# V of block 2 from raw rows, blocks 2 and 3 transposed by DMA from ScalarE's queue, block 3 loaded earlier

## The chip, the core and the metric

The kernel runs on one core of one Trainium2 chip. The metric is the device time of one execution in microseconds. An engine here is one of the core's: TensorE (PE, with its weight loads shown apart as PEld), VectorE (DVE), ScalarE (ACT), GpSimd (POOL) and SyncE (SP, which only issues transfers). All five run their own instruction lists in order and wait for one another by semaphores.

## What is computed

x has 2048 rows of 512 values. Two branches read the layer-normalised rows and are added to x.

```
xn = layernorm(x)
A:  q, k, v = xn @ wqkv           # 32 heads of 16
    for every row s and head: 8 logits, with rows s, s-2, ... s-14; softmax; weighted sum of v
    A = o @ wo
B:  z  = gelu(xn @ w_in)          # 1792 columns
    z1 = z[:, :896];  z2 = layernorm(z[:, 896:])
    g  = w_sp @ z2 + b_sp         # over the rows
    B = (z1 * g) @ w_out
out = x + A + B
```

## The kernel before

The rows are cut into 16 blocks of 128 (b = 0 to 15). For each block VectorE takes mean and variance (`bnst`, `bnag`, `vpe`: lines 599, 601, 609), GpSimd the reciprocal root (`rstd`, line 611), VectorE the normalised rows (`norm`, line 623). TensorE needs the normalised rows transposed (`xnT`). For blocks 0 to 3 (`NXT = 4`) TensorE transposes them itself by four small matmuls with an identity (`xTr`, line 579) and ScalarE copies the result out of PSUM (`xTe`, line 587). Blocks 4 to 15 are transposed by a DMA that SP issues (`xTd`, line 617).

From `xnT` come V (two pairs of matmuls a block, `V2_0` and `V2_1` for block 2, line 654), z2 (eight matmuls of 448 columns a block, `z2_2_0`, `z2_2_1`, line 766, followed by ScalarE's gelu `z2g`, line 774, which empties their two PSUM banks), and for groups j of four blocks Q and K (line 677), z1 (line 812). So Q and K of j = 0 need blocks 0 to 3 transposed.

Blocks 0 and 1 have a way round the wait for the norm: their V is computed from the raw rows. TensorE transposes the raw rows (`xTx`, also line 579), ScalarE copies them (`xTc`, line 606), and V of the raw rows is mended afterwards with the column sums of the weights (`cs`, line 638, copied by `cse`, line 642): VectorE adds mean times minus the column sum into the PSUM bank (`fix`, line 660), and ScalarE's `Ve` (line 663) scales by rstd, reorders into the head order and empties the bank. GpSimd's queue writes V to DRAM (`Vw`, line 668), from where it is read much later in shifted copies.

The order is made in two steps. Every operation is a task with an estimated cost and a priority; `schedule` runs a list scheduler on those estimates and on the landing times given for the first loads (`land`), and so fixes each engine's instruction list and the PSUM banks. There are eight banks, and `place` gives a task that needs two of them an even pair (0,1), (2,3), (4,5) or (6,7), once all users of the banks' last contents have been scheduled; a matmul group then waits for those users. Hand-written chains (lines 1003 to 1012) force parts of the order at the start: on TensorE, VectorE and ScalarE. A task that only issues a DMA is counted with 0.48 us on its engine (`issue`, line 128).

SP loads at the start, in its order: wv in two halves, x2, the two halves of w_in's second part (`ldwin2a`, `ldwin2b`, lines 524 and 530), x3 to x7, wq, wk, x8 to x15. ScalarE's queue loads x0 and x1.

## Time and profile before

| | |
|---|---|
| time, median of 3 runs | 237.26 us (237.21 to 237.38) |
| profiled execution, first to last instruction | 236.1 us |
| the rest of the time around the span (difference of the two) | 1.2 us |
| PE busy | 231.7 us (98%) |
| DVE busy | 207.4 us (88%) |
| ACT busy | 96.5 us (41%) |
| granted TensorE clock | 1.000 |

Times inside the span count from its first instruction. The busy time of TensorE is the sum of its matmuls, in which the end of each is modelled; where matmuls follow each other without a break, the start of the next is the better mark. In a list of instructions in order of time, the columns are start, duration (both in us), engine, line, operation, output and input, shape, how many instructions were merged, and in brackets the idle time before and what ended it.

### The profile page before, as it was taken

What the parts mean: (1) busy time and instruction counts of PE and PEld (TensorE: products, weight loads), DVE (VectorE), ACT (ScalarE), POOL (GpSimd) and SP (SyncE); (2) the same over time, 40 slices, a digit from 0 to 9 for tenths busy, and PEclk for the clock granted to TensorE, in tenths of its full rate; (3) what the DMA queues carried; (4) which work ended last, traced back from release to release, by engine and by line L of the source; (5) the groups of instructions that cost most, each with busy time, mean ns of one, the idle gap of its engine ahead of it and who ended that gap; (6) DMA issues with size and microseconds to landing.
All of it is one profiled execution on the core that took longest, in us unless ns stands there. A gap on an engine that the chain in (4) does not pass through costs nothing.

```text
span 236.1 us, 2974 instructions
## 1 busy us (share of the span) xinstructions
PE 231.7 (98%) x1114; PEld 109.1 (46%) x1135; DVE 207.4 (88%) x269; ACT 96.5 (41%) x145; POOL 32.7 (14%) x56
## 2 busy tenths in 40 slices
PE   8999999999999999999999999999999999999996
PEld 3455555555444444444444444444444444444443
DVE  3799899999998899999699998986989997999432
ACT  3598889888967895510120531111111111000000
POOL 2259650311733100000000000000000000000000
PEclk9999999999999999999999999999999999999999
DMA  7998969991048325430999999998995959936432
GB/s 211 352 283 163 243 146 217 195 202 44 22 165 260 92 85 69 104 118 0 226 347 252 225 266 180 200 304 187 346 258 175 261 161 303 193 95 181 135 96 69
DMA packets 82013, 43.86 MB, mean 186 GB/s; under 512 B 54336, under 2 KB 81360, under 8 KB 82000
## 3 DMA queue, kind: packets, MB, share of 16 engines
q1 hardware_dynamic: 80768, 41.27, 71.5%
q0 software_dynamic: 800, 2.11, 2.8%
q10 hardware_dynamic: 432, 0.30, 0.6%
q8 instruction: 9, 0.15, 0.3%
q14 instruction: 4, 0.03, 0.1%
HBM read 26.35 MB, written 4.21 MB: 129 GB/s over the span
## 4 chain that ended last, share of the span: by engine, by line
PE 94%; DMA 3%; SPq 1%; ACT 1%; issue 1%; DVE 0%
PE ps L907 41%; PE ps L677 12%; PE ps L972 10%; PE ps L812 10%; PE ps L766 9%; PE ps L963 6%; PE ps L654 5%; DMA arena<-in_B_w_in_dram 3%; PE ps L713 1%; ACT arena L774 0%; SPq L518 0%; ACT arena L587 0%; PE ps L579 0%; SPq L514 0%; SPq L524 0%
## 5 line engine op out<-in xcount | busy, mean ns | idle before, releaser
L907 PE MATMUL ps<-arena 128*128 128x512 bf16 x439 | 96.6, 379 | 0.5
L907 PEld LDWEIGHTS ps<-arena 128*128 128x128 bf16 x448 | 43.7, 98 | 53.1 <-issue 0.4
L915 ACT ACTIVATE arena<-ps 128x1024 bf16<-128x1024 f32 (+1 forms) x16 | 14.7, 917 | 78.0 <-PE ps L907 78.0
L698 DVE TENSOR_TENSOR arena<-arena 128x4096 bf16<-128x4096 bf16 x16 | 36.5, 2282 | 0.1
L935 DVE TENSOR_TENSOR arena<-arena 128x4096 bf16<-128x4096 bf16 x16 | 36.4, 2283 | 0.0
L938 DVE TENSOR_TENSOR arena<-arena 128x2048 bf16<-128x2048 bf16 (+1 forms) x32 | 29.9, 948 | 0.0
L677 PE MATMUL ps<-arena 128*128 128x512 bf16 x126 | 28.7, 379 | 0.1
L703 DVE TENSOR_TENSOR arena<-arena 128x4096 bf16<-128x4096 bf16 x12 | 27.4, 2287 | 0.1
L972 PE MATMUL ps<-arena 128*128 128x512 bf16 (+2 forms) x117 | 26.9, 366 | 0.1
L766 PE MATMUL ps<-arena 128*128 128x448 bf16 x128 | 26.0, 352 | 0.5 <-DMA arena<-in_B_w_in_dram 0.5
L812 PE MATMUL ps<-arena 128*128 128x512 bf16 x110 | 24.4, 379 | 0.1
L978 DVE TENSOR_TENSOR arena<-ps,arena 128x512 bf16<-128x512 f32 (+2 forms) x17 | 11.2, 658 | 11.7 <-PE ps L972 11.7
L677 PEld LDWEIGHTS ps<-arena 128*128 128x128 bf16 x128 | 14.5, 113 | 13.0
L766 PEld LDWEIGHTS ps<-arena 128*128 128x128 bf16 x128 | 12.3, 98 | 12.7 <-ACT arena L642 0.7
L686 ACT ACTIVATE arena<-ps 128x1024 bf16<-128x1024 f32 x16 | 16.3, 1021 | 4.4 <-PE ps L677 4.1
L972 PEld LDWEIGHTS ps<-arena 128*128 128x128 bf16 x119 | 11.4, 98 | 12.8
L812 PEld LDWEIGHTS ps<-arena 128*128 128x128 bf16 x112 | 10.9, 98 | 13.2 <-ACT arena L818 0.3
L963 PE MATMUL ps<-arena 128*128 128x512 bf16 (+2 forms) x66 | 16.5, 366 | 0.1
L774 ACT ACTIVATE arena<-ps 128x896 bf16<-128x896 f32 x16 | 14.6, 914 | 3.2 <-PE ps L766 3.1
L818 ACT ACTIVATE arena<-ps 128x1024 bf16<-128x1024 f32 (+1 forms) x16 | 13.9, 923 | 4.9 <-PE ps L812 4.8
L654 PE MATMUL ps<-arena 128*128 128x512 bf16 x60 | 15.6, 379 | 0.2
L779 ACT ACTIVATE arena<-arena 128x896 bf16<-128x896 bf16 x16 | 15.1, 945 | 0.0
(61 smaller groups left out, 168.5 us busy)
## 6 DMA issues: line engine op xcount, KB each, us to landing
arena<-vscr SPq DMA_DIRECT2D x16, 1024.0 KB, 7.1
arena<-in_A_x_dram SPq DMA_DIRECT2D x30, 128.0 KB, 3.6
vscr<-arena POOLq DMA_DIRECT2D x16, 128.0 KB, 3.0
out_dram<-arena SPq DMA_DIRECT2D x15, 128.0 KB, 1.8
arena<-in_A_wqkv_dram SPq DMA_DIRECT2D x2, 512.0 KB, 6.9
arena<-in_B_w_in_dram SPq DMA_DIRECT2D x2, 448.0 KB, 6.1
arena<-in_B_w_in_dram SPq DMA_DIRECT2D x1, 896.0 KB, 5.9
arena<-in_B_w_out_dram SPq DMA_DIRECT2D x1, 896.0 KB, 4.9
```

The lines of the kernel that those rows point to most:

```text
L654: last = t.matmul(P(bk, 512), A("xcT", 128, 512 * b + 128 * dc) if b < 2 else xTv(b, dc), A("wv", 512, 512 * dc), start=(dc == 0), stop=(d ...
L677: last = t.matmul(P(bk, 512, 512 * which), AC(off["wqk"] + 2048 * which + 512 * dc + c, [[4, 128]]), AC(off["xnT"] + dc * S + 512 * j, [[1 ...
L686: T("act", lambda a: a.activation(AC(qo, [[ko - qo, 2], [1, 512]]), P(bk, 1024).rearrange("p (t n) -> p t n", t=2), ACTF.Copy, scale=0.5), ...
L698: T("dve", (lambda pbv, qb, kb: lambda v: v.tensor_tensor(pbv, qb, kb, ALU.mult))(pbv, qb, kb), reads=rd, writes=[("pb", s_)], est=c_tt(40 ...
L703: T("dve", (lambda av, bv: lambda v: v.tensor_tensor(av, av, bv, ALU.add))(av, bv), reads=[("pb", 1)], writes=[("pb", acc)], est=c_tt(4096 ...
L766: last = t.matmul(P(bk, 448, 512 * hf), xTv(b, dc), AC(off["w_in2"] + 896 * dc + 448 * hf, [[1, 448]]), start=(dc == 0), stop=(dc == 3))
L812: last = t.matmul(P(bk, 512, 512 * i), AC(off["w_in1"] + 896 * dc + 128 * fc, [[1, 128]]), AC(off["xnT"] + dc * S + 512 * j, [[1, 512]]), ...
L907: last = t.matmul(P(bk, 512, 512 * i), AC(off["z2"] + FH * sh + 128 * fc, [[1, 128]]), AC(off["wT%d" % r_] + sh * 512, [[1, 512]]), start= ...
L935: T("dve", lambda v: v.tensor_tensor(tv, tv, av, ALU.mult), reads=[("attn", b)], writes=[("Vs", sv)], est=c_tt(4096), name="pv%d" % b, pri ...
L938: T("dve", (lambda n: lambda v: v.tensor_tensor(A("Vs", n, 4096 * sv), A("Vs", n, 4096 * sv), A("Vs", n, 4096 * sv + n), ALU.add))(n), wri ...
L963: last = t.matmul(P(bk, cn), AC(off["OT"] + 512 * tb + 128 * cc, [[1, 128]]), AC(off["wo"] + 512 * cc + c0, [[1, cn]]), start=(cc == 0), s ...
L972: last = t.matmul(P(bk, cn), AC(off["z1T"] + fc * S + 128 * tb, [[1, 128]]), AC(off["w_out"] + 512 * fc + c0, [[1, cn]]), start=False, sto ...
```

## The change

- `NRAW = 3`: V of block 2 is made from raw rows as well (`xTx2`, one `xTc2_0` of 512 columns, `V2_0`, `V2_1`, `fix2`), and on TensorE it now stands ahead of z2 of block 0.
- `NXT = 2`: the normalised blocks 2 and 3 are no longer transposed on TensorE (`xTr2`, `xTr3` and their copies `xTe2`, `xTe3` go); a DMA issued from ScalarE's queue transposes them (`xTd2`, `xTd3`). Block 4's transpose, from SP's queue, waits until both have landed, and block 5's and the later ones stand behind it.
- x3 is loaded ahead of the two halves of w_in's second part.
- `Ve` of blocks 0 to 2 scales and copies the bank into a new buffer `vraw` in 32-bit floats, without waiting for `fix`; `fix` then works from that buffer into the bf16 result, with a product mean times rstd that one more VectorE instruction (`mr`) makes.
- The raw copies, the column sums and `vraw` lie in another part of SBUF. The hand-written chains are new, the scheduler's tolerance is 20 instead of 50 ns and its VectorE overlap 20 instead of 40 ns, and the landing times are restated.

```diff
-    NXT = 4
+    NXT = 2
+    NRAW = 3
...
         ld_x(2, "sp")
+        ld_x(3, "sp")
         ld_win2a()
         ld_win2b()
-        ld_x(3, "sp")
...
-            return dma("sp", lambda e: e.dma_start_transpose(AC(off["xnT"] + 128 * b, [[S, 4], [1, 128]]), xn),
-                       128 * 512 * 2, ("xT", sl), reads=[("xn", sl)], writes=[("xnT", b)], name="xTd%d" % b,
+            return dma("act" if b < 4 else "sp", lambda e: e.dma_start_transpose(AC(off["xnT"] + 128 * b, [[S, 4], [1, 128]]), xn),
+                       128 * 512 * 2, ("xT", sl), reads=[("xn", sl)] + ([("turned", 2), ("turned", 3)] if b == 4 else []),
+                       writes=[("xnT", b)] + ([("turned", b)] if b < 4 else []), name="xTd%d" % b,
                        xbar=True, prio=1)
...
+        def mean_rstd():
+            T("dve", lambda v: v.tensor_tensor(Fv("mr", NRAW), Fv("mv", 2 * NRAW).rearrange("p (b t) -> p b t", t=2)[:, :, 0],
+                                               Fv("rstd", NRAW), ALU.mult),
...
-            if b < 2:
-                T("dve", lambda v: v.scalar_tensor_tensor(P(bk, 512), ncs, Fv("mv", 1, 2 * b), P(bk, 512),
-                                                          ALU.mult, ALU.add),
-                  reads=["ncs", ("mv", b)], writes=[bk], est=690, name="fix%d" % b, prio=1)
...
+            if b < NRAW:
+                T("act", lambda a: a.activation(vraw(b), P(bk, 512), ACTF.Copy, scale=Fv("rstd", 1, b)),
+                  reads=[bk, ("rstd", b)], writes=[("vraw", b)], est=c_act(512), name="Ve%d" % b, prio=4)
+                T("dve", lambda v: v.scalar_tensor_tensor(vdh, hd(ncs), Fv("mr", 1, b), hd(vraw(b)), ALU.mult, ALU.add),
+                  reads=["ncs", "mr", ("vraw", b)], writes=[("Vn", sl)], est=690, name="fix%d" % b, prio=1)
...
-                      ["xTx0", "cs_0", "V0_0", "xTx1", "cs_1", "V0_1", "xTr0", "V1_0", "xTr1", "V1_1",
-                       "z2_0_0", "z2_0_0b", "z2_0_1", "xTr2", "z2_1_0", "z2_1_1", "V2_0", "V2_1", "xTr3", "z2_2_0"],
+                      ["xTx0", "cs_0", "V0_0", "xTx1", "cs_1", "V0_1", "xTx2", "V1_0", "V1_1", "xTr0", "V2_0", "V2_1", "xTr1",
+                       "z2_0_0", "z2_0_0b", "z2_0_1", "z2_1_0", "z2_1_1", "z2_2_0"],
                       ("rstd4", "Vw0"),
...
+                      ("bnst0", "bnag0", "vpe0", "bnst1", "bnag1", "vpe1", "norm0", "bnst2", "norm1", "bnag2", "vpe2", "bnst3",
+                       "norm2", "bnag3", "vpe3", "norm3", "bnst4", "bnag4", "vpe4", "mr", "bnst5", "fix0", "fix1", "fix2"),
...
-                      ("xTc0_0", "xTc0_1", "xTc1_0", "xTc1_1", "xTe0_0", "xTe0_2", "cse", "xTe1_0", "xTe2_0", "z2g0",
-                       "Ve0", "xTe3_0", "z2g1", "Ve1", "Ve2", "z2s0"), ("V10_1", "Q3_3")):
+                      ("xTc0_0", "xTc0_1", "xTc1_0", "xTc1_1", "xTc2_0", "xTe0_0", "xTe0_2", "xTd2", "xTe1_0", "Ve1", "xTd3",
+                       "Ve0", "Ve2", "z2g0", "cse", "z2g1", "z2s0"), ("V10_1", "Q3_3")):
...
-        plan.schedule(tol=50.0, dma_bw=300.0, dma_lat=1600.0, overlap=40.0,
-                      land=dict(ldx0=3580.0, ldx1=4700.0, ldwv0=4050.0, ldwv1=5300.0, ldx2=5700.0, ldwin2a=6950.0, ldwin2b=8250.0,
-                                ldx3=8650.0, ldx4=9050.0, ldx5=9400.0, ldx6=9750.0, ldx7=10200.0, ldq=11700.0, ldk=13200.0))
+        plan.schedule(tol=20.0, dma_bw=300.0, dma_lat=1600.0, overlap=20.0,
+                      land=dict(ldx0=3690.0, ldx1=4590.0, ldwv0=4220.0, ldwv1=5320.0, ldx2=5680.0, ldwin2a=8450.0,
+                                ldwin2b=9650.0, ldx3=6040.0, ldx4=10060.0, ldx5=10440.0, ldx6=10820.0, ldx7=11250.0, ldq=12740.0, ldk=14220.0, xTd2=12000.0, xTd3=13300.0))
```

More of the change, by code (lines that the diff above doesn't have):

```diff
@@ L370, in build_kernel @@
     place(4 * S, xnT=0, OT=0)
-    place(3584, w_in1=0, tg=0, On=2048, xcT=0, ncs=1024)
+    place(3584, w_in1=0, tg=0, On=2048)
     place(3584, w_in2=0, w_out=0)
@@ L380, in build_kernel @@
     off["xn"] = off["attn"]
+    off["xcT"] = off["pb"] + 4096
+    off["ncs"] = off["xcT"] + 512 * NRAW
+    off["vraw"] = off["ncs"] + 1024
     AR = top[0]
@@ L386, in build_kernel @@
     for name, n in (("prime", 4), ("mx", 128), ("Zb", 256), ("Z", 128), ("maskt", 128), ("st6", NB * 6),
-                    ("mv", NB * 2), ("vpe", NB), ("rstd", NB), ("s1", NB), ("s2", NB), ("m2", NB), ("msq", NB),
+                    ("mv", NB * 2), ("vpe", NB), ("rstd", NB), ("s1", NB), ("s2", NB), ("m2", NB), ("msq", NB), ("mr", 4),
                     ("vpe2", NB), ("rstd2", NB), ("mhalf", 4)):
@@ L466, in build_kernel @@
         for hf in range(2):
-            for b in range(2):
+            for b in range(NRAW):
                 R1(("xcT", b, hf), "xcT", 256, 512 * b + 256 * hf)
@@ L470, in build_kernel @@
         R1("ncs", "ncs", 1024)
+        for b in range(NRAW):
+            R1(("vraw", b), "vraw", 1024, 1024 * b)
         R1("bbc", "bbc", S)
@@ L602, in ln_block @@
               writes=[("mv", b)], est=178, name="bnag%d" % b, prio=-1 + b * 0.1)
-            if b < 2:
+            if b < NRAW:
                 bc = pe_tr(xin, xk, "xTx%d" % b)
-                for hf in range(2):
-                    T("act", (lambda hf: lambda a: a.activation(A("xcT", 256, 512 * b + 256 * hf), P(bc, 256, 256 * hf),
-                                                                ACTF.Copy))(hf),
-                      reads=[bc], writes=[("xcT", b, hf)], est=c_act(256), name="xTc%d_%d" % (b, hf), prio=-1)
+                for h0, hn in ((0, 1), (1, 1)) if b < 2 else ((0, 2),):
+                    T("act", (lambda h0, hn: lambda a: a.activation(A("xcT", 256 * hn, 512 * b + 256 * h0),
+                                                                    P(bc, 256 * hn, 256 * h0), ACTF.Copy))(h0, hn),
+                      reads=[bc], writes=[("xcT", b, hf) for hf in range(h0, h0 + hn)], est=c_act(256 * hn),
+                      name="xTc%d_%d" % (b, h0), prio=-1)
             T("dve", lambda v: v.tensor_scalar(Fv("vpe", 1, b), Fv("mv", 1, 2 * b + 1), LN_EPS, None, ALU.add),
@@ L640, in mm, with vraw, hd @@
                     return last
-                T("pe", mm, reads=[("wv", hf)], writes=[bk], est=2 * c_mm(512) * (1 if hf else 2), name="cs_%d" % hf, prio=2)
+                T("pe", mm, reads=[("wv", hf)], writes=[bk], est=2 * c_mm(512) * (1 if hf else 1.6), name="cs_%d" % hf, prio=2)
             T("act", lambda a: a.activation(ncs, P(bk, 512), ACTF.Copy, scale=-1.0), reads=[bk],
               writes=["ncs"], est=c_act(512), name="cse", prio=-0.5)
+        def vraw(b):
+            return A("vraw", 1024, 1024 * b).bitcast(F32)
+        def hd(x):
+            return x.rearrange("p (h d) -> p d h", d=16)
+        def mean_rstd():
+            T("dve", lambda v: v.tensor_tensor(Fv("mr", NRAW), Fv("mv", 2 * NRAW).rearrange("p (b t) -> p b t", t=2)[:, :, 0],
+                                               Fv("rstd", NRAW), ALU.mult),
+              reads=[("mv", b) for b in range(NRAW)] + [("rstd", b) for b in range(NRAW)], writes=["mr"], est=160,
+              name="mr", prio=1)
         def v_block(b):
@@ L653, in mm @@
                     for dc in (2 * hf, 2 * hf + 1):
-                        last = t.matmul(P(bk, 512), A("xcT", 128, 512 * b + 128 * dc) if b < 2 else xTv(b, dc),
+                        last = t.matmul(P(bk, 512), A("xcT", 128, 512 * b + 128 * dc) if b < NRAW else xTv(b, dc),
                                         A("wv", 512, 512 * dc), start=(dc == 0), stop=(dc == 3))
                     return last
-                T("pe", mm, reads=[("xcT", b, hf) if b < 2 else ("xnT", b), ("wv", hf)], writes=[bk],
-                  est=2 * c_mm(512) * (1.5 if (b, hf) == (0, 0) else 1), name="V%d_%d" % (b, hf), prio=(2 if b < 4 else 60 + b))
-            if b < 2:
-                T("dve", lambda v: v.scalar_tensor_tensor(P(bk, 512), ncs, Fv("mv", 1, 2 * b), P(bk, 512),
-                                                          ALU.mult, ALU.add),
-                  reads=["ncs", ("mv", b)], writes=[bk], est=690, name="fix%d" % b, prio=1)
-            T("act", lambda a: a.activation(vn.rearrange("p (d h) -> p d h", d=16),
-                                            PC(bk.col(), [[1, 16], [16, 32]]), ACTF.Copy,
-                                            scale=Fv("rstd", 1, b) if b < 2 else 1.0),
-              reads=[bk] + ([("rstd", b)] if b < 2 else []), writes=[("Vn", sl)], est=c_act(512), name="Ve%d" % b,
-              prio=4)
+                T("pe", mm, reads=[("xcT", b, hf) if b < NRAW else ("xnT", b), ("wv", hf)], writes=[bk],
+                  est=2 * c_mm(512) , name="V%d_%d" % (b, hf), prio=(2 if b < 4 else 60 + b))
+            vdh = vn.rearrange("p (d h) -> p d h", d=16)
+            if b < NRAW:
+                T("act", lambda a: a.activation(vraw(b), P(bk, 512), ACTF.Copy, scale=Fv("rstd", 1, b)),
+                  reads=[bk, ("rstd", b)], writes=[("vraw", b)], est=c_act(512), name="Ve%d" % b, prio=4)
+                T("dve", lambda v: v.scalar_tensor_tensor(vdh, hd(ncs), Fv("mr", 1, b), hd(vraw(b)), ALU.mult, ALU.add),
+                  reads=["ncs", "mr", ("vraw", b)], writes=[("Vn", sl)], est=690, name="fix%d" % b, prio=1)
+            else:
+                T("act", lambda a: a.activation(vdh, PC(bk.col(), [[1, 16], [16, 32]]), ACTF.Copy),
+                  reads=[bk], writes=[("Vn", sl)], est=c_act(512), name="Ve%d" % b, prio=4)
             dma("pool", lambda e: e.dma_start(vscr[16 + 128 * b: 16 + 128 * b + 128, :], vn),
@@ L825, in build_kernel @@
             lastx = ld_x(b)
-        lnd = [ln_block(b) for b in range(2)]
+        lnd = [ln_block(b) for b in range(NRAW)]
+        mean_rstd()
         colsum()
-        v_block(0)
-        v_block(1)
-        lnd += [ln_block(b) for b in range(2, NB)]
+        for b in range(NRAW):
+            v_block(b)
+        lnd += [ln_block(b) for b in range(NRAW, NB)]
         dma("pool", lambda e: e.dma_start(vscr[0:16, :], ar[0:16, off["zeros"]: off["zeros"] + 512]), 16 * 512 * 2,
@@ L847, in build_kernel @@
               after=lnr[:8])
-        for b in range(2, NB):
+        for b in range(NRAW, NB):
             v_block(b)
@@ L873, in build_kernel @@
                                                              ap=[[0, 128], [1, S]])),
-            128 * S * 2, "bbc", writes=["bbc"], name="ldbbc", prio=7, after=lnd[NXT:])
+            128 * S * 2, "bbc", writes=["bbc"], name="ldbbc", prio=7, after=lnd[4:])
         def ld_wT(tc):
@@ L882, in ld_wT @@
                     128 * S * 2, ("wT", p_), writes=[("wTs", r_, p_)], name="wT%d_%d" % (tc, p_), xbar=True,
-                    prio=6 + tc, after=lnd[NXT:])
+                    prio=6 + tc, after=lnd[4:])
         dma("sp", lambda e: e.dma_start(A("w_out", FC * 512).rearrange("p (c n) -> p c n", c=FC),
@@ L1003, in build_kernel @@
         for names in (["warm%d" % wi for wi in range(NWARM)] +
-                      ["xTx0", "cs_0", "V0_0", "xTx1", "cs_1", "V0_1", "xTr0", "V1_0", "xTr1", "V1_1",
-                       "z2_0_0", "z2_0_0b", "z2_0_1", "xTr2", "z2_1_0", "z2_1_1", "V2_0", "V2_1", "xTr3", "z2_2_0"],
+                      ["xTx0", "cs_0", "V0_0", "xTx1", "cs_1", "V0_1", "xTx2", "V1_0", "V1_1", "xTr0", "V2_0", "V2_1", "xTr1",
+                       "z2_0_0", "z2_0_0b", "z2_0_1", "z2_1_0", "z2_1_1", "z2_2_0"],
                       ("rstd4", "Vw0"),
-                      ("bnst0", "bnag0", "vpe0", "bnst1", "bnag1", "vpe1", "norm0", "norm1", "bnst2", "bnag2",
-                       "vpe2", "norm2", "fix0", "bnst3", "bnag3", "vpe3", "fix1", "norm3", "bnst4", "bnag4", "vpe4",
-                       "bnst5"),
+                      ("bnst0", "bnag0", "vpe0", "bnst1", "bnag1", "vpe1", "norm0", "bnst2", "norm1", "bnag2", "vpe2", "bnst3",
+                       "norm2", "bnag3", "vpe3", "norm3", "bnst4", "bnag4", "vpe4", "mr", "bnst5", "fix0", "fix1", "fix2"),
                       ["bnst%d" % b for b in range(5, NB)],
-                      ("xTc0_0", "xTc0_1", "xTc1_0", "xTc1_1", "xTe0_0", "xTe0_2", "cse", "xTe1_0", "xTe2_0", "z2g0",
-                       "Ve0", "xTe3_0", "z2g1", "Ve1", "Ve2", "z2s0"), ("V10_1", "Q3_3")):
+                      ("xTc0_0", "xTc0_1", "xTc1_0", "xTc1_1", "xTc2_0", "xTe0_0", "xTe0_2", "xTd2", "xTe1_0", "Ve1", "xTd3",
+                       "Ve0", "Ve2", "z2g0", "cse", "z2g1", "z2s0"), ("V10_1", "Q3_3")):
             for n0, n1 in zip(names, names[1:]):
```

## The prediction, made before the changed kernel ran

> **What bounds the kernel now.** I read the page's busy times and its chain of waits first, then TensorE's instructions in order of time.

> ```profile
> PE 231.7 (98%) x1114; PEld 109.1 (46%) x1135; DVE 207.4 (88%) x269; ACT 96.5 (41%) x145; POOL 32.7 (14%) x56
> ...
> PE 94%; DMA 3%; SPq 1%; ACT 1%; issue 1%; DVE 0%
> ```

> TensorE is busy 98% of the span and carries 94% of the chain; the 3% of DMA is one load, w_in's second part. So time goes only where TensorE stands still or has less to do. Its list around the change:

> ```profile
> 7.34 0.59 PE L654 MATMUL ps<-arena 128*128 128x512 bf16 x2
> 8.22 0.92 PE L766 MATMUL ps<-arena 128*128 128x448 bf16 x4 [0.28 <-DMA arena<-in_B_w_in_dram]
> 9.34 0.93 PE L766 MATMUL ps<-arena 128*128 128x448 bf16 x4 [0.21 <-DMA arena<-in_B_w_in_dram]
> 10.11 0.39 PE L579 MATMUL ps<-arena 128*128 128x128 bf16 x4
> 10.33 1.68 PE L766 MATMUL ps<-arena 128*128 128x448 bf16 x8
> 12.06 0.81 PE L654 MATMUL ps<-arena 128*128 128x512 bf16 x3
> 12.71 0.39 PE L579 MATMUL ps<-arena 128*128 128x128 bf16 x4
> 12.93 1.68 PE L766 MATMUL ps<-arena 128*128 128x448 bf16 x8
> 14.45 1.03 PE L654 MATMUL ps<-arena 128*128 128x512 bf16 x4
> ```

> Read starts, not durations: the distance of starts gives 0.86 us for four matmuls of 512 columns (14.45 to 15.31, where Q begins), 1.51 for eight of 448 (12.93 to 14.45), 0.22 for a transpose (12.71 to 12.93). V of block 1 is over at 7.34 + 0.43 = 7.77, but z2 begins at 8.22; its first half is over at 8.98, its second begins at 9.34. These two waits, 0.45 + 0.37 = 0.82 us, are for the two halves of w_in's second part (landed at 8.09 and 9.30). Behind 9.34 I find no standstill of TensorE above 0.1 us up to the end. So the mark is the start of block 3's V: 14.45. From there both kernels have the same work for TensorE, and **the time changes by as much as that start moves, plus any new hole behind it**.

> **TensorE's part.** Two transposes go and one comes: -0.22. V2 (0.86, at 11.85 before, with one record missing) moves ahead of z2. Now follow TensorE with unchanged starts up to V0_1, which ends at 6.46: xTx2 to 6.69, V1 to 7.55, xTr0 to 7.77, V2 to 8.63, xTr1 to 8.86, first half of z2 of block 0 to 9.61. x2 landed at 5.68 and is there in time. x3 ahead of w_in's halves delays these by one load of 128 KB; consecutive x loads landed 0.31 to 0.43 apart (9.75, 10.07, 10.44, 10.82, 11.25), so about 8.5 and 9.7: the first is hidden, the second costs 0.13, and z2 of block 0 ends at 10.50. If nothing else waited, z2 of blocks 1 and 2 would end at 13.52, against 14.45: **0.93 gained at most**.

> **ScalarE's part.** The two transposes are issued in ScalarE's list. What that costs stands nowhere in ScalarE's rows; the nearest rows are SP's transposes of the same form and ScalarE's own load of x0:

> ```profile
> L617 SPq DMA_TRANSPOSE arena<-arena x12: 1189/1266/1647, 14.5 to 30.0; - x12
> ...
> DMA to landing us min/median/max: 2.4/4.3/5.9
> ```

> ```profile
> L541 ACTq DMA_DIRECT2D arena<-in_A_x_dram x1: 420/420/420, 0.8 to 0.8; - x1
> ```

> The columns are least, median and largest duration in ns. Bounds: 0.42 by ScalarE's plain load, 1.65 by SP's longest transpose. I take 1.27: SP's plain loads take 0.43 to 0.51, as ScalarE's do, so it is the form that makes the issue long, not the queue. The planner counts 0.48.

> Next, whether the issue lies beside ScalarE's previous instruction. The sequencer's records show a semaphore wait of ScalarE at 63.896, 8 ns after the ACTIVATE at 63.888 had begun and 0.9 before it ended, and never one before the previous instruction began. So I let an issue begin with the ACTIVATE ahead of it, and the one behind wait for its end. The next durations come from ScalarE's list:

> ```profile
> 7.43 0.60 ACT L642 ACTIVATE arena<-ps 128x512 f32<-128x512 f32 x1
> 7.91 0.62 ACT L587 ACTIVATE arena<-ps 128x512 bf16<-128x512 f32 x1
> ...
> 15.55 0.68 ACT L663 ACTIVATE arena<-ps,fpool 128x512 bf16<-128x512 f32 x1
> 16.12 1.08 ACT L663 ACTIVATE arena<-ps 128x512 bf16<-128x512 f32 x2
> ```

> A copy of 512 columns takes 0.60, the next begins 0.48 behind its start; with a scale 0.68 and 0.57. By VectorE's durations (0.69 statistics, 0.18, 0.15, GpSimd's 0.55 for rstd, norm 0.41), norm2 is over at 8.40, norm3 at 9.75. In ScalarE's list: xTe0_2 begins at 8.26; **xTd2** issues 8.42 to 9.69; xTe1 9.72 to 10.32; Ve1 10.20 to 10.88; **xTd3** 10.22 to 11.49; Ve0 11.52 to 12.20; Ve2 12.09 to 12.77; z2g0, 1.0 with its accumulator read, to 13.7; then the column sums to 14.2.

> Who waits for these: TensorE, for PSUM banks. I follow `place` by hand. The column sums and V0 hold banks 2 and 3, V1 is in 6, V2 in 0, xTr1 in 1; z2 of block 0 gets 4 and 5. z2 of block 1 then can have only (6,7), once Ve1 has emptied V1; z2 of block 2 only (0,1), once Ve2 has emptied V2. With 0.12 from a copy's end to the matmul behind (norm1's end at 7.00 to the transpose at 7.12), z2 of block 1 runs 11.00 to 12.51, z2 of block 2 starts at max(12.51, 12.77 + 0.12) = 12.89 and ends at 14.40. So 0.5 of the gain is lost to Ve1 and 0.38 to Ve2. xTe2 and xTe3 (0.60 each), which go, lay beside TensorE's work and give nothing.

> **The landings.** Block 2's transpose is needed at 12.89, block 3's at 14.40. From issue to landing the row gives 2.4 (queue empty, 28.7) to 5.9 (behind the load of w_in1, 20.8); 4.9 at 14.5, behind the last x loads. From ScalarE's queue there is no line to stand in, but from 8 to 14 us SP's loads keep all engines full. GpSimd's V writes, also 128 KB on a queue of their own, took 3.9 beside those loads and 3.0 in the median, 1.9 at best; adding 1.4, between the excesses 0.9 and 2.0, to 2.4 gives 3.8: landings at 12.2 and 14.0, both just in time. The loads of x4 to wk give way by up to the 0.6 that each transpose's packets take alone; K needs wk, which landed at 14.22, at 16.1: hidden.

> [...]

> **VectorE's and GpSimd's part.** fix2 adds 0.75 (row of line 660) and mr 0.15; fix0 to fix2 now wait for the column sums, at 14.2. Behind them stand norms of blocks 4 and up; block 7's transpose landed at 21.81 and was needed at 25.24. The first reduction for the logits (64.64) had 1.45 to spare behind VectorE. Cost nothing, unless the cover goes: then up to 0.9. Block 4's transpose, issued at 14.49 before, now waits for 14.0: no change.

> **Sum**: -0.82 waits, +0.13 new load wait, -0.22 transpose, +0.86 banks (0.50 + 0.38, less rounding): 14.40 against 14.45, -0.05. On the timed median: 237.26 - 0.05 = **237.2**. The span (236.1) stands 1.2 below the median; what lies around it I keep.

> **Rivals.**
> - Cheap issue, faster. At 0.42 on ScalarE, Ve1 ends at 10.2, ahead of TensorE (10.50); xTd3 waits for norm3 and issues at 9.77; Ve2 ends at 11.5, and z2 of block 2 follows block 2's landing, 12.2: 12.25 to 13.76. xTd3 lands at 13.6. -0.69: 236.6. For it: ScalarE's own row. Against: all 12 transposes took 1.19 or more. [...] Chance 0.22.
> - Late landing, slower. Block 3's transpose decides from 14.40 - 10.22 = 4.2 us on: V, z2 and Q, K of j = 0 all need block 3, so nothing can fill in. At 4.9: 15.17, +0.72: 238.0; at 5.9, 239.0. For: full DMA engines, the median of 4.3. Against: those medians stood in SP's line. Chance 0.16.
> - The issue begins only when ScalarE's previous copy has ended, slower: xTd2 8.66 to 9.93, Ve1 to 11.12, xTd3 11.14 to 12.41, Ve2 to 13.69, z2 of block 2 from 13.81 to 15.32: +0.87, 238.1. Against: the wait records. An issue that queues behind SP's would look alike, but at 0.80 both queues issued side by side in 0.42 and 0.46. [...] Chance 0.12.
> - The list behind is sorted anew, and TensorE, without a hole before, gets one, from VectorE or ScalarE: +0.2 to 1, 237.9 or so. Chance 0.10, of which 0.02 stays within the bound.

> That the change doesn't do what it says is excluded for the start: the hand-written chain forces V2 ahead of z2.

> **Numbers.** 0.2% is 0.47 us, about what a measurement of this kernel can tell from no change. Forecast 0.40, its own range 236.9 to 237.6. Faster by over 0.2%: 0.22; within: 0.40 + 0.02 = 0.42; slower: 0.16 + 0.12 + 0.08 = 0.36. The range takes in the fast rival and the slow ones up to 238.2, and leaves out the landings near 5.9 and an issue still cheaper: 236.5 to 238.2.

> **What would show it.** Right: two transposes of about 1.27 on ScalarE's queue near 8.4 and 10.2; L766 at 9.7, 11.0 and 12.9, the last two released by ScalarE; L654 of block 3 at 14.4. Wrong: a wait of L654 near 14.4 for a transpose; L766 without a wait for ScalarE; a break in TensorE's list behind 15 us.

## The result, and the profile after

The changed kernel takes 242.65 us (median of 6 runs, 241.01 to 243.61); the kernel before, beside it, 237.19 (6 runs, 236.94 to 237.38). The ratio is 1.0226 [1.0205, 1.0246]: 5.5 us slower, where 237.2 was forecast and 238.2 was the end of the range. The profiled execution took 243.33 us with a span of 242.0.

From the page of the changed kernel: busy times, granted clock in 40 slices, chain of waits by engine.

```profile
PE 234.9 (97%) x1131; PEld 109.5 (45%) x1131; DVE 209.0 (86%) x271; ACT 96.5 (40%) x144; POOL 33.1 (14%) x56
...
PEclk9977999999999999999999999999999999999999
...
PE 92%; DMA 4%; DVE 2%; POOL 0%; issue 0%; DVEq 0%
```

Two things stand out against the page of before. TensorE is busy 3.2 us longer, although its work hardly changed, and slices 3 and 4 (12 to 24 us) show a granted clock below full. In the chain, the share of the DMA (4%) is no longer w_in: 3% is the transposes (`DMA arena<-arena`).

TensorE's instructions in order of time. The lines have moved: L674 is V (L654 before), L786 z2 (L766), L697 Q and K (L677), L585 the transposes by TensorE (L579).

```profile
7.53 1.03 PE L674 MATMUL ps<-arena 128*128 128x512 bf16 x4
8.40 0.39 PE L585 MATMUL ps<-arena 128*128 128x128 bf16 x4
8.62 1.68 PE L786 MATMUL ps<-arena 128*128 128x448 bf16 x8
10.89 1.69 PE L786 MATMUL ps<-arena 128*128 128x448 bf16 x8 [0.60 <-ACT arena L681]
16.29 3.17 PE L786 MATMUL ps<-arena 128*128 128x448 bf16 x8 [3.71 <-DMA arena<-arena]
19.25 1.91 PE L674 MATMUL ps<-arena 128*128 128x512 bf16 x4
20.96 7.34 PE L697 MATMUL ps<-arena 128*128 128x512 bf16 x32
28.13 3.19 PE L786 MATMUL ps<-arena 128*128 128x448 bf16 x16
```

V of block 3, my mark, starts at 19.25 instead of 14.45 (forecast 14.40), and Q at 20.96 instead of 15.31. TensorE's last matmul then ends at 240.1 instead of 234.2, 5.9 later. So nearly all is lost ahead of Q, in two pieces:

- **A standstill.** z2 of block 1 is over at 12.40 (10.89 and 1.51). z2 of block 2 begins at 16.29, released by a DMA from the arena to the arena: block 2's transpose. 3.9 us.
- **Half speed.** Behind it z2 of block 2 takes 2.96 (16.29 to 19.25) instead of 1.51, V 1.71 instead of 0.86, and the first Q and K 7.17 (20.96 to 28.13) instead of 6.9: 2.6 more.

Ahead of Q the sum is 3.89 + 2.30 (2.96 - 1.51 and 1.71 - 0.86) + 0.76 (10.13 to 10.89, a bank that ScalarE's Ve1 empties) - 0.82 (waits for w_in) - 0.22 (one transpose fewer) - 0.24 (the list began that much earlier in this execution: V of block 0 was over at 6.22, and at 6.46 before) = 5.67; Q moved by 5.65.

The table of stretches of the changed kernel: us, busy time (and number) of PE, PEld, DVE, ACT, POOL, then the granted clock, the DMA share and GB/s.

```profile
8.30:12.50 4.20, 3.60 (x22) 1.61 (x19) 3.43 (x13) 2.78 (x6) 1.10 (x2) 1.00 1.08 360
12.50:14.60 2.10, 0.08 (x1) 0.00 (x0) 2.07 (x6) 2.04 (x5) 1.20 (x2) 1.00 1.16 255
14.60:21.50 6.90, 5.21 (x14) 2.05 (x15) 3.53 (x11) 1.31 (x3) 1.40 (x3) 0.51 0.96 155
21.50:28.00 6.50, 6.50 (x32) 3.40 (x31) 4.01 (x11) 5.01 (x8) 5.27 (x19) 1.00 0.60 148
```

The clock is 0.51 in the third stretch and 1.00 on both sides; the clock's own records give half from 14.66 to 21.48.

Now the transposes. ScalarE's list (ACTq is its sequencer):

```profile
8.31 1.30 ACTq L624 DMA_TRANSPOSE arena<-arena  x1
9.66 0.60 ACT L593 ACTIVATE arena<-ps 128x512 bf16<-128x512 f32 x1 [1.27 <-DVE arena L631]
9.71 1.22 ACTq L624 DMA_TRANSPOSE arena<-arena  x1
10.15 0.68 ACT L681 ACTIVATE arena<-ps,fpool 128x512 f32<-128x512 f32 x1
10.99 1.27 ACT L681 ACTIVATE arena<-ps,fpool 128x512 f32<-128x512 f32 x2
```

Block 2's is issued when the prediction said (8.42), block 3's 0.5 us earlier than it said (10.22), and both issues take what it said (1.27). But block 2's lands at 16.25 and block 3's at 17.70, **7.9 and 8.0 us after the issue**. The transfers of the changed kernel from 8.3 to 12.5 us, and then from 12.5 to 16.3 (queue: packets, MB, share of 16 engines, where the times of packets overlap, so that it can pass 100%; q10 is ScalarE's, q1 is SP's):

```profile
DMA packets 1569, 1.51 MB, mean 360 GB/s; under 512 B 90, under 2 KB 1569, under 8 KB 1569
...
q1 hardware_dynamic: 1569, 1.51, 107.7%
...
arena<-arena ACTq DMA_TRANSPOSE x2, 8.0
```

```profile
DMA packets 1701, 0.85 MB, mean 223 GB/s; under 512 B 1128, under 2 KB 1701, under 8 KB 1701
...
q1 hardware_dynamic: 644, 0.59, 78.2%
q10 hardware_dynamic: 1057, 0.26, 39.3%
```

For 4.2 us after the issue q10 sends no packet at all. Then its packets of 256 B go out beside the x loads, and all together move 223 GB/s instead of 360. So there are two questions: what holds the transposes back, and what halves the clock.

### The profile page after: what moved, and what is told of

The parts are those of the page before. It is cut to its first block, busy times and chain, and to the rows that moved or that the text cites. A ratio compares the mean times of both kernels' runs of the same rounds, so it can differ in the third digit from the quotient of the medians.

```text
span 242.0 us, 2996 instructions
## 1 busy us (share of the span) xinstructions
PE 234.9 (97%) x1131; PEld 109.5 (45%) x1131; DVE 209.0 (86%) x271; ACT 96.5 (40%) x144; POOL 33.1 (14%) x56
## 4 chain that ended last, share of the span: by engine, by line
PE 92%; DMA 4%; DVE 2%; POOL 0%; issue 0%; DVEq 0%
PE ps L928 40%; PE ps L697 12%; PE ps L832 10%; PE ps L993 10%; PE ps L786 9%; PE ps L984 6%; PE ps L674 5%; DMA arena<-arena 3%; DMA arena<-in_A_x_dram 1%; PE ps L733 1%; DVE fpool L605 1%; DVE arena L631 0%; DVE arena L999 0%; POOL fpool L618 0%; DVE fpool L607 0%; DVE fpool L616 0%
## 5 line engine op out<-in xcount | busy, mean ns | idle before, releaser
L928 PE MATMUL ps<-arena 128*128 128x512 bf16 x448 | 97.0, 379 | 0.0
L786 PE MATMUL ps<-arena 128*128 128x448 bf16 x128 | 27.3, 367 | 4.3 <-DMA arena<-arena 3.7
L697 PE MATMUL ps<-arena 128*128 128x512 bf16 x128 | 29.2, 381 | 0.0
L832 PE MATMUL ps<-arena 128*128 128x512 bf16 x112 | 24.5, 379 | 0.0
L697 PEld LDWEIGHTS ps<-arena 128*128 128x128 bf16 x128 | 14.6, 114 | 13.6 <-issue 0.6
L786 PEld LDWEIGHTS ps<-arena 128*128 128x128 bf16 x128 | 12.7, 101 | 17.4 <-DMA arena<-arena 4.2
L706 ACT ACTIVATE arena<-ps 128x1024 bf16<-128x1024 f32 x16 | 16.3, 1021 | 4.2 <-PE ps L697 3.9
L832 PEld LDWEIGHTS ps<-arena 128*128 128x128 bf16 x112 | 10.9, 98 | 13.3 <-ACT arena L838 0.3
L674 PE MATMUL ps<-arena 128*128 128x512 bf16 x64 | 16.8, 395 | 0.0
L939 DVE TENSOR_TENSOR arena<-arena 128x1024 bf16<-128x1024 bf16 (+1 forms) x16 | 9.9, 621 | 6.7 <-ACT arena L936 6.6
```

Source lines behind the costliest of these rows:

```text
L674: last = t.matmul(P(bk, 512), A("xcT", 128, 512 * b + 128 * dc) if b < NRAW else xTv(b, dc), A("wv", 512, 512 * dc), start=(dc == 0), stop ...
L697: last = t.matmul(P(bk, 512, 512 * which), AC(off["wqk"] + 2048 * which + 512 * dc + c, [[4, 128]]), AC(off["xnT"] + dc * S + 512 * j, [[1 ...
L706: T("act", lambda a: a.activation(AC(qo, [[ko - qo, 2], [1, 512]]), P(bk, 1024).rearrange("p (t n) -> p t n", t=2), ACTF.Copy, scale=0.5), ...
L786: last = t.matmul(P(bk, 448, 512 * hf), xTv(b, dc), AC(off["w_in2"] + 896 * dc + 448 * hf, [[1, 448]]), start=(dc == 0), stop=(dc == 3))
L832: last = t.matmul(P(bk, 512, 512 * i), AC(off["w_in1"] + 896 * dc + 128 * fc, [[1, 128]]), AC(off["xnT"] + dc * S + 512 * j, [[1, 512]]), ...
L928: last = t.matmul(P(bk, 512, 512 * i), AC(off["z2"] + FH * sh + 128 * fc, [[1, 128]]), AC(off["wT%d" % r_] + sh * 512, [[1, 512]]), start= ...
```

## The experiments

**The theory, "one line":** a transfer's packets go out only when what any queue issued earlier has been sent. Ahead of block 2's transpose SP had issued 3.41 MB in all (issues that were over by then); the first transpose packet left at 12.58 us, when 3.41 MB had been sent. **First rival:** ScalarE's queue itself, or a transpose from it, is slow. **Second rival:** only transposes wait, not plain loads. **Third rival:** the transposes stand back for the other queue's loads altogether, those issued later too. And for the clock: the standstill halves it, or else something in the new code does.

All kernels are the changed kernel with the edit shown, except e12, which is the kernel before. Three dots stand for lines left out: the hand-written chains and the planner's landing times that follow from the edit, and the rest of a long line. Where an expectation has letters for theories, they are its own.

**e1: blocks 2 and 3 transposed by TensorE again, the rest of the change kept.**

```diff
-    NXT = 2
+    NXT = 4
...
-                        "z2_0_0", "z2_0_0b", "z2_0_1", "z2_1_0", "z2_1_1", "z2_2_0"],
+                        "z2_0_0", "z2_0_0b", "z2_0_1", "z2_1_0", "xTr2", "z2_1_1", "xTr3", "z2_2_0", "z2_2_1", "V3_0"],
...
```

> The change without its transposes by DMA: blocks 2 and 3 are transposed by TensorE again, all other parts stay (V of block 2 from raw rows ahead of z2, x3 loaded earlier, the new fix). Theory (the late landing of blocks 2 and 3 is the whole loss): V of block 3 begins at about 14.1 us, against 14.45 in the kernel before, no hole behind it, 236.7 to 237.1 us. Rival (the other parts, or the order behind that is sorted anew, cost time as well): holes behind 15 us, 239 us or more.

Measured: 237.34 (10 runs, 236.69 to 237.88) against 237.14 (13 runs, 236.64 to 237.39), ratio 1.0007 [0.9996, 1.0018], where 236.7 to 237.1 was expected. So the whole loss sits in the two transposes by DMA. In the profile (236.98) the waits for w_in are gone and Q starts at 14.87, 0.44 ahead of before; but the median shows no gain. That is taken up below (e9 to e12).

**e5: the changed kernel with 14 matmuls of constants between z2 of block 1 and of block 2**, whose result nobody reads.

```diff
+        bx = plan.bank("warmx")
+        for wi in range(14):
+            T("pe", lambda t: t.matmul(P(bx, 512), ones[:, 0:128], ones[:, 0:512], start=True, stop=True),
+              writes=[bx], est=1.0, name="warmx%d" % wi, prio=3)
...
```

> The changed kernel with 14 idle matmuls (3.0 us, on constants) between z2 of block 1 and z2 of block 2, where TensorE waits; the order of all else is the same. Theory (the wait is followed by a stretch at half the granted clock, because TensorE stood still): the transposes land as late as in the changed kernel, about 16.2 us, the granted clock is 1.00 in every run, 240.7 to 241.3 us with hardly any spread. Rival (the half clock has nothing to do with the wait): clock 0.986 to 0.993 again, 242 to 243.6 us.

Measured: 240.84 (4 runs, 240.76 to 241.05), ratio 1.0157 [1.014, 1.0174], granted clock 1.000 in all four. TensorE's list of e5 (here L791 is z2, L679 V, L702 Q and K):

```profile
12.68 3.01 PE L572 MATMUL ps<-const-bfloat16-1.0 128*128 128x512 bf16 x13
16.23 1.67 PE L791 MATMUL ps<-arena 128*128 128x448 bf16 x8 [0.55 <-DMA arena<-arena]
17.83 1.04 PE L679 MATMUL ps<-arena 128*128 128x512 bf16 x4
18.70 6.64 PE L702 MATMUL ps<-arena 128*128 128x512 bf16 x29
```

The transpose lands as late as before (16.10), but eight matmuls of z2 now take 1.60, and Q starts at 18.70 instead of 20.96. Idle matmuls make the kernel 1.8 us faster. With the standstill filled, none of four runs had a granted clock below 1.000; with it, five of the changed kernel's six had 0.986 or 0.993. So that share is measured.

**e4: wq, wk and x8 to x15 issued only when block 3's transpose has landed.** Of SP's loads only w_in's second half and x4 to x7 are then in front.

```diff
+        byname["ldq"].deps.add(byname["xTd3"])
+        names = ["ldq", "ldk"] + ["ldx%d" % b for b in range(8, 16)]
+        for n0, n1 in zip(names, names[1:]):
+            byname[n1].odeps.add(byname[n0])
...
```

> The changed kernel with the loads of wq, wk and x8 to x15 held on SP until block 3's transpose has landed; in front of block 2's transpose there are then only w_in's second half and x4 to x7, which landed by 10.5 us. Theory (the transposes wait for and share the DMA engines with SP's loads): block 2's transpose lands at 11 to 12.5 us, and block 3's at 12.5 to 14; z2 of block 2 is released by ScalarE at about 12.9; Q and K then wait for wq. Rival (a transpose issued from ScalarE's queue is slow of itself): 7.9 us from issue to landing again, 16.2 us. The time is worse in both, since wq and wk come late.

Measured: 237.70 (one run). Issues at 8.47 and 9.84, landings at 11.27 and 12.16: 2.8 and 2.3 us. TensorE's list of e4:

```profile
11.01 3.20 PE L786 MATMUL ps<-arena 128*128 128x448 bf16 x16 [0.24 <-ACT arena L681]
14.26 0.81 PE L674 MATMUL ps<-arena 128*128 128x512 bf16 x3
14.91 1.68 PE L786 MATMUL ps<-arena 128*128 128x448 bf16 x8
16.43 7.07 PE L697 MATMUL ps<-arena 128*128 128x512 bf16 x32
23.88 1.30 PE L786 MATMUL ps<-arena 128*128 128x448 bf16 x6 [0.39 <-DMA arena<-arena]
```

x16 in the first line is z2 of blocks 1 and 2 without a break. The standstill is gone, with the same queue and the same instructions: the first rival falls. The price comes not at Q, as expected, but later, at 23.88, where z2 of block 4 waits for its transpose, issued behind the held loads.

**e6: two late transposes (blocks 14 and 15) also from ScalarE's queue**, when little is under way.

```diff
-            return dma("act" if b < 4 else "sp", lambda e: e.dma_start_transpose(
+            return dma("act" if b < 4 or b >= 14 else "sp", lambda e: e.dma_start_transpose(
...
```

> The changed kernel with the transposes of blocks 14 and 15 issued from ScalarE's queue as well, after those of SP have landed, at about 35 us when hardly any load runs. Theory (SP's loads make the landing late): 2.4 to 2.8 us from issue to landing there, and again about 7.9 for block 2. Rival (ScalarE's queue is slow of itself): 5 us or more there too.

Measured: 240.91 (one run). At 34.05 and 35.30 the same instruction lands after 2.34 and 2.43 us, while block 2's again takes 8.0 (8.32 to 16.35). Against the first rival once more. The granted clock stayed at 1.00 here, in spite of a standstill of 4 us; see the last section.

**e3: only x8 to x15 held until block 3's transpose has landed; wq and wk stay ahead.**

```diff
+        byname["ldx8"].deps.add(byname["xTd3"])
...
```

> The changed kernel with the loads of x8 to x15 held on SP until block 3's transpose has landed; wq and wk still stand in front. In the changed kernel the first packet of block 2's transpose went out at 12.6 us, when SP's queue had sent 3.4 MB, which is all that SP had issued before the transpose. Theory (a transpose waits until the loads issued before it have gone, and only then shares the engines): first packet at about 12.2 us, when SP's queue has sent the 3.28 MB up to wk; landings at about 13.4 and 14.3, z2 of block 2 at 13.4. Rival (it only shares the engines with whatever runs beside it, from its issue on): packets from 9.5 us on, between those of wq and wk, landing before 12.5.

Measured: 239.18 (one run). The first packet left at 11.85; the rival (packets from 9.5 on) falls.

**e2: the transposes issued by SP, behind wk and ahead of x8.**

```diff
-            return dma("act" if b < 4 else "sp", lambda e: e.dma_start_transpose(
+            return dma("sp", lambda e: e.dma_start_transpose(
...
+        names = ["ldk", "xTd2", "xTd3"] + ["ldx%d" % b for b in range(8, 16)]
...
```

> The changed kernel with the transposes of blocks 2 and 3 issued by SP, behind wk and ahead of x8. Theory (they wait for all that was issued before): no difference between the queues: first packet at about 12.2 us, landings at 13.4 to 14.5. Since ScalarE no longer issues them, z2 of block 1 begins without a wait for ScalarE, at about 10.3 instead of 10.9. Rival (a line of its own lets ScalarE's transposes start earlier than SP's): landings later than in the kernel with x8 to x15 held.

Measured: 240.40 (one run, granted clock 0.993). The first packet left at 11.75 and the transposes landed earlier than e3's, not later; the time is worse than e3's, and the clock's records show half from 15.03 to 18.44 here.

**e8: a plain load (x9) from ScalarE's queue, just ahead of block 2's transpose.**

```diff
-            lastx = ld_x(b)
+            lastx = ld_x(b, "act" if b == 9 else "sp")
...
```

> The changed kernel with the load of x9 issued from ScalarE's queue, directly ahead of block 2's transpose. It is a plain load of 128 KB, as the transposes are 128 KB. Theory A (only a transpose waits for what was issued before, a plain load interleaves): x9 lands within 2.9 to 4 us of its issue, about 11.2 to 12.3. Theory B (any transfer waits for what was issued before it): x9 lands at 13.5 us or later. Block 2's transpose lands at about 16 us in both.

Measured: 244.14 (one run, granted clock 0.986). x9 landed at 14.25, 6.0 us after its issue, as theory B has it; block 2's transpose, now behind x9 as well, landed at 16.95.

**e7: SP issues the transposes between x7 and wq, and z2 of block 3 goes ahead of Q**, so that wq and wk may come later.

```diff
-            return dma("act" if b < 4 else "sp", lambda e: e.dma_start_transpose(
+            return dma("sp", lambda e: e.dma_start_transpose(
...
+        names = (["ldx7", "xTd2", "xTd3", "ldq", "ldk", "ldx8", "ldx9", "ldx10", "ldx11", "xTd4", "ldx12", "ldx13", "xTd5",
+                  "ldx14", "ldx15", "xTd6"])
+        for n0, n1 in list(zip(names, names[1:])) + [("z2_3_1", "Q0_%d" % c) for c in range(4)]:
+            byname[n1].odeps.add(byname[n0])
...
```

> A version made from the theory: SP issues the transposes of blocks 2 and 3 between x7 and wq, wq, wk and x8 to x15 follow, and z2 of block 3 stands ahead of Q. In front of the transposes only w_in's second half and x4 to x7 are left. Theory: landings at about 11.3 and 12.2 us, no wait of TensorE for ScalarE at z2 of blocks 1 and 2, V of block 3 at 13.2 to 13.5 instead of 14.45; 236.0 to 236.5 us if no hole opens behind. Rival (the loads given back later: Q waits for wq and wk, or the late transposes of blocks 4 to 7 for their place behind them): a hole near 15 or 23 us, 236.8 us or more.

These four together with e4 give a series in one quantity: how many bytes SP had issued ahead.

| kernel | queue of the transposes | issued by SP ahead of the issue, MB | sent when the first packet left, MB | first packet, us | landings, us | time, us |
|---|---|---|---|---|---|---|
| changed | ScalarE | 3.41 | 3.41 | 12.58 | 16.25, 17.70 | 242.65 |
| e8 (its plain load) | ScalarE | 3.41 | 3.24 | 12.14 | 14.25 | 244.14 |
| e3 | ScalarE | 3.28 | 3.08 | 11.85 | 14.13, 14.60 | 239.18 |
| e2 | SP | 3.28 | 3.15 | 11.75 | 13.90, 14.40 | 240.40 |
| e4 | ScalarE | 2.23 | 2.20 | 9.71 | 11.27, 12.16 | 237.70 |
| e7 | SP | 2.23 | 2.18 | 9.49 | 10.93, 11.91 | 237.04 |

All these issues began between 8.22 and 8.47. The first packet leaves when 94 to 100% of what had been issued ahead is sent; e2 and e3, which differ in the queue, agree within 0.25 us; a plain load waits like a transpose, so the second rival falls. The last two rows say less than the others: their first packets left 1.24 and 1.27 us after the issue began, and with little under way (e6 at 34.05) it took 1.19, so they hardly waited. They show that the wait goes when the bytes ahead go; its size is shown by the four rows above. The third rival falls with the changed kernel itself: the packets begin at 12.6, while the later x loads go on to 18.5.

The theory of one line holds in the main, but the order is not strict: e3's first packet left with 0.19 MB of what stood ahead unsent, and e8's x9 landed at 14.25, before x8 (14.56), which SP had issued 0.98 us earlier. What makes the line, the engines or what feeds them, no run here shows. Of the 2.9 us between e4's first packet and the changed kernel's, 2.1 go with wq and wk (e3 less e4) and 0.7 with x8 (changed less e3). The landings of e3 came later than expected (13.4 and 14.3). TensorE in e3 and in e2:

```profile
10.80 1.69 PE L786 MATMUL ps<-arena 128*128 128x448 bf16 x8 [0.53 <-ACT arena L681]
14.17 1.69 PE L786 MATMUL ps<-arena 128*128 128x448 bf16 x8 [1.69 <-DMA arena<-arena]
```

```profile
8.74 3.19 PE L786 MATMUL ps<-arena 128*128 128x448 bf16 x16
13.95 0.93 PE L786 MATMUL ps<-arena 128*128 128x448 bf16 x4 [2.02 <-DMA arena<-arena]
```

In e2 z2 of blocks 0 and 1 run as one group of 16: without the issues on ScalarE, Ve1 empties its bank in time. So the bank wait that the prediction counted (0.60 in the changed kernel) does come from the issues.

e7 has everything that the change can give. Its TensorE list:

```profile
9.25 4.70 PE L786 MATMUL ps<-arena 128*128 128x448 bf16 x24
14.01 0.81 PE L674 MATMUL ps<-arena 128*128 128x512 bf16 x3
14.65 1.68 PE L786 MATMUL ps<-arena 128*128 128x448 bf16 x8
16.17 0.81 PE L697 MATMUL ps<-arena 128*128 128x512 bf16 x3
```

No wait stands in it. Yet it takes 237.04 (11 runs, 236.60 to 237.64) against 237.13 (15 runs, 236.42 to 237.36), ratio 0.9996 [0.9986, 1.0007], where 236.0 to 236.5 was expected. The landings came earlier than expected (11.3 and 12.2), V of block 3 at 14.01 later (13.2 to 13.5): its first z2 starts at 9.25, in the changed kernel at 8.62.

**e9, e10 (e1 again), e11 (e7 again), e12 (the kernel before again): one more profiled execution each**, to see where the gain of e1 and e7 went.

> The kernel with blocks 2 and 3 transposed by TensorE once more, for one more profiled execution. Its timed executions spread from 236.69 to 237.88 us, its first profile (236.98) had TensorE without a break from 3.56 us on, Q at 14.87 and 218.89 us from there to TensorE's end. Theory 'the beginning moves': from Q's start to TensorE's end it is again 218.8 to 219.0, and the span differs from 235.66 only as far as the first z2 starts before or after 8.91 (between 8.6 and 9.9), later when TensorE's full clock is granted later. Rival 'something behind': the first z2 starts within 0.1 of 8.91 and the span differs by a standstill behind Q.

> The same kernel a third time, same expectation: from Q's start to TensorE's end 218.8 to 219.0; the span follows the start of the first z2, which lies between 8.6 and 9.9. Rival: the first z2 within 0.1 of 8.91 and a standstill behind Q.

> The kernel whose transposes are issued by SyncE ahead of wq, for a second profiled execution (the first: first z2 at 9.25, span 235.48, time 237.04). Theory 'the beginning moves': the span less the start of the first z2 is again 226.2 (225.9 to 226.5), and with a first z2 at 8.6 the span would be 234.9. What lies around the span is again 1.5 to 1.6 against 1.25 of the kernel before. Rival: the first z2 at 9.2 to 9.3 again and a standstill behind it.

> The kernel before, for a second profiled execution (the first: first z2 at 8.22, waits of 0.45 and 0.37 for the halves of w_in, Q at 15.31, span 236.06). If the beginning of TensorE's list moves here too but is absorbed by the waits for w_in, V of block 1 ends at another time than 7.77 while the second half of z2 of block 0 still starts within 0.2 of 9.34 or where w_in's second half lands, and from Q to TensorE's end it is again 218.8 to 219.0. Rival: the waits move with the beginning, and nothing is absorbed.

| execution | full clock from | first z2 | Q | Q to TensorE's end | span | time |
|---|---|---|---|---|---|---|
| e1 | 5.10 | 8.91 | 14.87 | 218.89 | 235.66 | 236.98 |
| e9 | no record | 9.52 | 15.48 | 218.89 | 236.27 | 237.61 |
| e10 | 3.57 | 8.46 | 14.42 | 218.89 | 235.21 | 236.55 |
| e7 | no record | 9.25 | 16.17 | 217.41 | 235.48 | 237.04 |
| e11 | no record | 9.24 | 16.16 | 217.41 | 235.47 | 237.04 |
| before | 4.79 | 8.22 | 15.31 | 218.87 | 236.06 | 237.26 |
| e12 | 4.57 | 8.01 | 15.10 | 218.87 | 235.86 | 237.09 |

(In e7 z2 of block 3, 1.51, lies ahead of Q; with it 218.92.) Behind Q every execution is the same to 0.05 us; what varies is the beginning. The lists of e10 and of e9:

```profile
4.06 0.60 PE L646 MATMUL ps<-arena,const-bfloat16-1.0 128*128 128x512 bf16 x2
4.50 0.59 PE L674 MATMUL ps<-arena 128*128 128x512 bf16 x2
4.93 0.39 PE L585 MATMUL ps<-arena 128*128 128x128 bf16 x4
```

```profile
4.05 1.04 PE L646 MATMUL ps<-arena,const-bfloat16-1.0 128*128 128x512 bf16 x2
4.88 1.06 PE L674 MATMUL ps<-arena 128*128 128x512 bf16 x2
5.74 0.63 PE L585 MATMUL ps<-arena 128*128 128x128 bf16 x4
```

The same column sums, V and transposes take 0.6, 0.6 and 0.4 in one and 1.0, 1.1 and 0.6 in the other: e9 still runs them at about half the speed. "The beginning moves" holds for e1 (8.46 lies a little ahead of the range expected). For e11 it had nothing to explain, as its beginning came out the same. Without the waits for w_in nothing absorbs a late grant (Q follows the first z2 by 5.96 in e1, e9 and e10 alike), and the median of e1's spans is 236.05, against 235.9 of before. That before absorbs it with these waits would fit its narrower spans (235.4 to 236.1 beside e1's 235.4 to 236.6), but it isn't shown: its two profiled executions both had an early grant, and there the load of w_in's first half landed 0.21 apart (8.09, 7.88), as much as the spans differ. In e12 V of block 1 ended at 7.58 and the second half of z2 began at 9.13, both about 0.2 earlier than in the first profile; as the load moved too, e12 doesn't decide between its theory and its rival.

For e7 there is a second part. Its spans have a median of 235.5, 0.4 better than before. But what lies around the span is 1.53 to 1.64 in its 11 runs, and 1.18 to 1.30 in those of the kernel before. e2 and e3 have 1.6 as well, e4 1.45, e1 and the changed kernel 1.3, e8 1.24. No run shows what makes it; it stays open. The prediction kept this part as it was.

## Why the prediction was wrong

- **Waits for w_in, -0.82: right.** z2 of block 0 begins right behind the transpose, at 8.62, and its two halves run as one group. The load wait of 0.13 did not come: w_in's second half landed at 9.03, not 9.7.
- **Issue of a transpose on ScalarE, 1.27: right** (1.30 and 1.22), though of the plain loads of SP that it was compared with four took 0.59 to 0.99, not 0.43 to 0.51. The run-ahead goes further than the prediction let it: block 2's was issued at 8.31, ahead of the previous copy's end at 8.39, and block 3's at 9.71, not at 10.22, which is 0.44 before the instruction ahead of it in ScalarE's list (Ve1, 10.15) began. So the first rival (0.42) and the third (an issue that waits for the previous copy to end: xTd2 8.66) fall.
- **Ve1's bank, z2 of block 1 at 11.00: right**, 10.89, released by ScalarE's line 681. Ve2's bank never decided: z2 of block 2 came much later for another reason.
- **VectorE and GpSimd at nothing, no hole behind Q: right.** From Q to TensorE's end it is 219.14, and 218.87 before; the 0.27 is the last of the half clock.
- **The landings: the step that failed.** "From ScalarE's queue there is no line to stand in", it says, and takes 3.8 us (bounds 2.4 to 5.9). It was 7.9. I took a queue of its own to be a line of its own, and sized the rest by GpSimd's writes, which go out by another kind of queue (q0, software_dynamic on the page, where q1 and q10 are hardware_dynamic); no run here shows whether those stand in the same line. The size was to be had from the trace of before: by 8.42, where the prediction has the issue, SP had issued 3.41 MB (with x8, whose issue was under way) and sent 1.84, and at the 356 GB/s of that trace (8 to 14 us) the 1.57 MB in between take 4.4 us. SP's first transpose there took another 3.6 from its first packet (15.77) to its landing (19.41). That gives 8.0; measured were 4.3 and 3.7.
- **Two issues side by side proved too little.** The prediction held against a line that at 0.80 both queues issued side by side, in 0.42 and 0.46. From 3 to 4 us of that trace packets of both queues do go out, 252 of q1 and 153 of q10. But the loads on q10 were issued at 0.80 and 1.25, before the first 1 KB packet of either queue had gone (1.87); they don't tell what happens to one issued 8 us in, behind a backlog. In the changed kernel the two queues share the engines too (78.2% and 39.3% from 12.5 to 16.3 us), but a later issue does not start at once: in the 4.2 us from 8.3 to 12.5 not one packet of q10 went between the 1569 of q1.
- **The rival "late landing"** named the right place, but not the cause: it spoke of full DMA engines, held SP's line against itself, priced the time to 239.0 us at most and gave it 0.16. It also had block 3's transpose decide; TensorE stood still for block 2's, needed at 12.89 by the prediction and landed at 16.25.
- **The clock was missed altogether.** The prediction treats a standstill as lost time and no more. Here 3.9 us of standstill cost another 2.6 behind it. At the granted clock of 1.00 the changed kernel took 241.01, with 0.993 241.8 to 242.7, with 0.986 243.3 to 243.6.

## What to carry to other kernels

Issue a transfer that the start of a chain needs ahead of the bulk loads, not beside them from another engine: issued ahead (e7) the two transposes landed at 10.93 and 11.91, beside (changed) at 16.25 and 17.70. Where that can't be, count the bytes issued and not yet sent, divide by the rate, and add it to the landing: here 1.57 MB at 356 GB/s, 4.4 us, where 4.3 were measured. A standstill of TensorE can cost more than itself: here half clock followed for 3.4 us behind a standstill of 2.2 (e2), for 6.8 behind one of 3.9 (changed), and not at all behind one of 4.0 (e6). And a wait at the beginning that is taken away may have been hiding a jitter of the same size, which was not shown here: compare the spread of the times, not one profile.

## What the runs showed of the hardware

| kernel | full clock from | stretch | busy in it | clock behind it |
|---|---|---|---|---|
| changed | 4.42 | 11.25 to 14.66 | 1.2 | half |
| changed | | 14.66 to 18.07 | 1.8 | half still |
| e2 | 4.79 | 11.62 to 15.03 | 1.2 | half |
| e2 | | 15.03 to 18.44 | 3.4 | full |
| e8 | 5.50 | 12.32 to 15.74 | 0.4 | half |
| e8 | | 15.74 to 19.15 | 2.2 | half still |
| e6 | 4.22 | 11.04 to 14.46 | 1.3 | full |
| e6 | | 14.46 to 17.87 | 1.5 | full |

So e2's standstill of 2.2 us cost it half the clock for 3.4 us, while e6's of 4.0, split evenly over two stretches, cost it none. Of the five rows that begin at full clock, half clock followed 0.4, 1.2 and 1.2 us of busy time, and full clock 1.3 and 1.5; of the three that begin at half, half clock stayed behind 1.8 and 2.2, and full clock came back behind 3.4. Whether the busy time of a stretch decides the clock of the next, no run here shows. The grant of full clock came at 4.22 to 5.50 in these four executions. Whether a standstill's place in the stretches makes the 2.6 us over which the times of the changed kernel spread was not shown: only one of these executions was traced.
